# Attention with a memory beside a gated FFN: half blocks of gate and up in row tiles, set-up moved, another order at the end

## The chip, the cores and the metric

The kernel runs on one core of a Trainium2 chip. The metric is device time in microseconds for the whole program, as a median over runs. A profile of one execution is shown beside it.

## The reference, cut to what matters

`x` is 2048 x 448. It is layer-normalised once; both branches read the result.

```python
xn = layernorm(x)
# branch A: 16 heads of 28 features, 4 segments of 512 rows in turn
q, k, v = xn @ wq, xn @ wk, xn @ wv
for s in range(4):
    p = softmax(q_s @ k_s.T * scale + causal_mask)
    a_dot = p @ v_s
    a_mem = (phi(q_s) @ M) / (phi(q_s) @ z + 1e-6)
    o_s = g * a_mem + (1 - g) * a_dot          # g = sigmoid(beta), per head
    M, z = M + phi(k_s).T @ v_s, z + sum(phi(k_s))
s_out = o @ wo
# branch B: w_gate, w_up 448 x 1792, w_down 1792 x 448
ffn = (gelu(xn @ w_gate) * (xn @ w_up)) @ w_down
out = x + s_out * silu(ffn)
```

## The kernel before, in words

All matmuls are bf16 into float32 PSUM. The 448 features stand as `NDC` = 4 chunks of 128 partitions, of which the last holds `DR` = 64 features and 64 rows of zeros. A segment's normalised rows, transposed, are `xnT[s]` (128 x 4 x 512).

The order of all instructions is written out by hand (`manual_schedule`, L79): each engine runs its instructions in the order in which the program issues them. Work goes in stages:

- **Head** (`layer_norm_first`, L265): constants and loads, statistics and transposes of segment 0 by TensorE (`turn`, L253), the four v units between them, then the eight q and k units (`run(units0[:8])`, L623). VectorE writes all set-up zeros first: `fill_constants` (L147) stands ahead of `stats`. 145 matmuls on zeros (L92, L93) keep TensorE at work until then. wq is spread to 32 columns a head by ACT, wk by VectorE (`pad_weight`, L118). `more_loads` (L135) starts the loads of gate, up, down and wo.
- **gate_up(s)** (L477), for s = 0 to 3: 14 blocks `fc` of 128 of the 1792 columns. A block's tile `gu` has two PSUM banks, one for gate and one for up, and there are two such tiles (`ps_s`, shared with the scores). Per block four matmuls for gate and four for up (L484), each 128 rows x 128 weights x 512 columns, then gelu on ACT (L487), the product on VectorE (L488) into `hT[s]`, and then the steps that a table holds for that block: statistics of the next segment (`layer_norm_steps`, L284), the end of the previous attention (`tail`, L632), reads of the memory (`memory`, L637).
- **attention(s, fill, at)** (L556): twelve steps (4 groups of 4 heads x 3 sets of key blocks). Scores are 32-row matmuls, four beside each other in row tiles (L388), exponentials on ACT (L394), the causal mask on GpSimd (L398), PV two steps later in 32-column tiles (L409). A list of other TensorE work (`fill`: q, k, v units, down units, wo units) is dealt out between by estimated costs, and `at` holds steps by half step (24 of them).
- A softmax or memory denominator is gathered by DMA into `dc` (L426), turned into three bf16 terms (`invert`, L435: VectorE, then casts and subtractions on GpSimd or VectorE), sent by DMA into `rows` (L448), and spread over the partitions by a matmul with `spread` (`inverses`, L456). `combine` (L463) and `scale_memory` (L459) multiply by it. This matmul reads all of `rows`, so it waits for every earlier write of it.
- `down_units(s)` (L493): per block of 128 rows 14 matmuls (L499) in five units of 3, 3, 3, 3 and 2, tanh on ACT, a product on VectorE. `finish_units(s)` (L522): four wo matmuls (L528), product and addition, store.
- **End** (L674 to L692): attention 2 carries two of the 20 down units of segment 2, attention 3 the other 18 and two of segment 3. The 18 left over run after it with a table of steps; then the last combine, and the four wo units with their additions on VectorE.

Of the kernel before, what the change touches and what calls it, by code (L numbers as in the profile page):

```python
# [25 lines left out]
def fast_path(tc, A_x, A_wq, A_wk, A_wv, A_wo, A_beta, B_w_gate, B_w_up, B_w_down, out):  # L26
# [16 lines left out]
    with ExitStack() as ctx:  # L43
# [48 lines left out]
        for i in range(145):  # L92
            nc.tensor.matmul(out=idle[:, 0:P], lhsT=wz[:], rhs=wz[:], start=True, stop=True)  # L93
        xns = []
        for i in range(2):
            xns.append(const.tile([P, NDC * P], BF16, name=f"xn{i}"))
            nc.vector.memset(xns[i][:, D:], 0.0)
# [5 lines left out]
        wu_sb = const.tile([P, NDC, F], BF16, name="wu_sb")  # L103
# [14 lines left out]
        def pad_weight(nm):  # L118
            copy = nc.scalar.copy if nm == "wq" else nc.vector.tensor_copy
            copy(out=wpad[nm][:, :, :, 0:Dh], in_=raw[nm][:].rearrange("p c (h d) -> p c h d", d=Dh))  # L120
# [14 lines left out]
        def more_loads():  # L135
            w_dma(nc.sync, wg_sb, B_w_gate)
            w_dma(nc.scalar, wu_sb, B_w_up)
# [4 lines left out]
            nc.sync.dma_start(out=wd_sb[:], in_=B_w_down.rearrange("(c p) n -> p c n", p=P))  # L142
            wo_v = A_wo.rearrange("(g i d) n -> i d g n", i=HG, d=Dh)
            for i in range(HG):
                nc.sync.dma_start(out=wo_sb[i * HP:i * HP + Dh, :, :], in_=wo_v[i])

        def fill_constants():  # L147
            nc.vector.memset(wo_sb[:], 0.0)
            for i in range(2):
                nc.vector.memset(vaug[i][:, :, :, Dh:HP], 0.0)  # L150
                nc.vector.memset(vaug[i][:, :, :, Dh:Dh + 1], 1.0)
            for t in (wg_sb, wu_sb):
                nc.vector.memset(t[DR:P, NDC - 1, :], 0.0)
# [35 lines left out]
        def flush():  # L189

            while waiting:
                tick()
# [37 lines left out]
        def layer_norm(s):  # L230
# [21 lines left out]

            def turn(b):  # L253
# [11 lines left out]
        def layer_norm_first():  # L265
# [3 lines left out]
            fill_constants()  # L269
            pad_weight("wq")  # L270
            for b in range(NB):
                stats(b)
            more_loads()
            units0.extend(project_units(0))
            v = units0[8:]
            for b in range(NB):
                scale_x(b)
                turn(b)
                if b:
                    run(v[b - 1:b])  # L280
            pad_weight("wk")
            run(v[NB - 1:])
# [194 lines left out]
        def gate_up(s, steps):  # L477

            hT[s] = seg2.tile([P, NFC, L], BF16, name="hT")
            for fc in range(NFC):  # L480
                gu = ps_s.tile([P, 2, L], F32, name="s")
                for i, w_sb in enumerate((wg_sb, wu_sb)):
                    for c in range(NDC):
                        nc.tensor.matmul(out=gu[:, i, :], lhsT=w_sb[:, c, fc * P:(fc + 1) * P],  # L484
                                         rhs=xnT[s][:, c, :], start=(c == 0), stop=(c == NDC - 1))
# [137 lines left out]
        run(units0[:8])  # L623
        check = guard()
# [7 lines left out]
        def tail(s, table, ends, n_inv, n_comb, copy=None):  # L632
            in_turn(table, 0, [ends[0], lambda: ends[1](copy)])
            in_turn(table, n_inv, [lambda: invert(s, 0)])
            return in_turn(table, n_comb, [lambda g=g: combine(s, g) for g in range(G)])

        def memory(s, table, n_read, n_inv, n_scale, copy=None):  # L637
            in_turn(table, n_read, [lambda g=g: memory_read(s, g, copy) for g in range(G)])
            in_turn(table, n_inv, [lambda: invert(s, 1)])
# [33 lines left out]
        for s in (2, 3):  # L673
# [3 lines left out]
        ends = attention(2, merge(pu[8:12], pu[:8], finish_units(1)) + d2[:2])  # L677
        at = memory(3, tail(2, {}, ends, 4, 9), 5, 13, 17)
        ends = attention(3, d2[2:] + merge(finish_units(2), d3[:2]), at)
        rest, n = d3[2:], 0  # L680
        fast = dict(eng=nc.vector, queues=[nc.sync, nc.scalar, nc.gpsimd])
        table = {0: [lambda: invert(3, 0, 0, G - 1, nc.vector)], 1: ends[:1], 3: ends[1:],
                 8: [lambda: invert(3, 0, G - 1, G, **fast)]}
        in_turn(table, 6, [lambda g=g: combine(3, g) for g in range(G - 1)])
# [4 lines left out]
        flush()  # L689
        combine(3, G - 1)  # L690
        run(finish_units(3))
        flush()  # L692
# [383 lines left out]
```

## Time and profile before

| | us |
|---|---|
| median of three runs | 295.4 (294.34 to 296.16) |
| the profiled execution | 295.26 |
| its span, from first to last instruction | 293.4 |
| TensorE busy (matmuls) | 261.4 |
| VectorE, ACT, GpSimd busy | 185.5, 157.8, 100.1 |

Engines: PE is TensorE, PEld its weight loads, DVE VectorE, ACT ScalarE, POOL GpSimd, SP SyncE; a name with q is that engine's DMA queue. Lines (L484) are those of the kernel. The profile's slices cut the span into 40 equal parts and give busy tenths; PEclk is TensorE's granted clock in tenths of full speed. The time of a matmul in a row includes its way through the array, so matmuls that follow each other overlap in the records; the distance of their starts is what each costs.

### The profile page before, as it was taken

To read this page: it belongs to the slowest core of one execution; us is meant where nothing else is said; L and a number is where in the kernel's file an instruction comes from. 1 tells how busy PE (TensorE), PEld (TensorE's weight loads), DVE (VectorE), ACT (ScalarE), POOL (GpSimd) and SP (SyncE) were. 2 spreads that over 40 slices of the span, in tenths; PEclk is the share of its full clock that TensorE was granted. 3 is DMA by queue.
4 is the path that set the end of the run, shared out by engine and by line. 5 is a ranking of instruction groups with operands and counts; after the bars stand their busy time and mean duration, and the time that the engine had idled before them with its cause. 6 is when DMAs were issued, how large, how long until landed. Compare 5 with 4: busy or idle time off the path is not lost. (4 is left out here: it accounts for less than half of the span.)

```text
span 293.4 us, 4695 instructions
## 1 busy us (share of the span) xinstructions
PE 261.4 (89%) x1697; PEld 116.9 (40%) x1697; DVE 185.5 (63%) x352; ACT 157.8 (54%) x227; POOL 100.1 (34%) x212
## 2 busy tenths in 40 slices
PE   7789799999999999999999999998999886873770
PEld 7634344433434345444444445443334332231330
DVE  6648666537786787478867654467772585566253
ACT  2338582688985325788853344339896765610000
POOL 4200000145540400976502151304776547550000
PEclk9999999999999999999999999999999998897596
DMA  7997012101010142011110300002000000010002
GB/s 230 349 326 155 19 36 53 49 0 21 19 29 17 29 93 92 12 40 36 35 21 7 72 1 6 7 0 80 17 19 19 4 12 8 32 37 3 2 2 70
DMA packets 26354, 15.11 MB, mean 51 GB/s; under 512 B 17872, under 2 KB 25044, under 8 KB 26324
## 3 DMA queue, kind: packets, MB, share of 16 engines
q1 hardware_dynamic: 23392, 10.20, 14.2%
q10 hardware_dynamic: 2324, 3.16, 3.4%
q0 software_dynamic: 608, 1.38, 1.3%
q8 instruction: 15, 0.25, 0.3%
q14 instruction: 15, 0.12, 0.1%
HBM read 9.18 MB, written 1.84 MB: 38 GB/s over the span
## 5 line engine op out<-in xcount | busy, mean ns | idle before, releaser
L394 ACT ACTIVATE pt<-s 128x1024 bf16<-128x1024 f32 (+1 forms) x96 | 79.3, 886 | 20.1 <-PE s L388 17.9
L398 POOL TENSOR_SCALAR_AFFINE_SELECT pt<-pt 128x256 bf16<-128x256 bf16 x128 | 53.6, 442 | 81.1 <-ACT pt L394 79.6
L487 ACT ACTIVATE gl<-s 128x512 bf16<-128x512 f32 x56 | 33.3, 597 | 58.9 <-PE s L484 41.2
L488 DVE TENSOR_TENSOR hT<-gl,s 128x512 bf16<-128x512 bf16 x56 | 38.5, 687 | 38.1 <-ACT gl L487 37.5
L484 PE MATMUL s<-xnT,wg_sb 128*128 128x512 bf16 x224 | 57.5, 379 | 2.2 <-DVE hT L488 2.2
L484 PE MATMUL s<-xnT,wu_sb 128*128 128x512 bf16 x224 | 57.5, 379 | 0.0
L499 PE MATMUL m<-wd_sb,hT 128*128 128x448 bf16 x224 | 53.9, 375 | 0.0
L484 PEld LDWEIGHTS <-wg_sb 128*128 128x128 bf16 x224 | 21.7, 98 | 28.2 <-issue 3.3
L484 PEld LDWEIGHTS <-wu_sb 128*128 128x128 bf16 x224 | 21.9, 98 | 26.4
L499 PEld LDWEIGHTS <-hT 128*128 128x128 bf16 x224 | 21.4, 102 | 24.4 <-issue 8.5
L388 PE MATMUL s<-qT,kT 32*128 32x512 bf16 (+3 forms) x256 | 22.2, 305 | 3.8 <-ACT pt L394 3.3
L246 POOL TENSOR_TENSOR rstd<-rstd,nhalf 128x2 f32<-128x2 f32 x8 | 5.7, 711 | 50.4 <-DVE rstd L244 50.4
L502 ACT ACTIVATE th<-m 128x448 f32<-128x448 f32 x16 | 8.8, 547 | 25.7 <-PE m L499 25.7
L456 PE MATMUL m<-rows,spread 128*128 128x512 bf16 x28 | 11.5, 417 | 12.2 <-DMA rows<-terms 10.6
L409 PE MATMUL pv<-pt,vaug 128*32 128x512 bf16 (+3 forms) x256 | 17.5, 311 | 0.0
L528 PE MATMUL m<-wo_sb,oT 128*128 128x448 bf16 x64 | 15.0, 355 | 2.3 <-DVE oT L473 1.9
L388 PEld LDWEIGHTS <-kT 32*128 32x128 bf16 x256 | 6.8, 91 | 25.6 <-issue 25.1
L307 PE MATMUL m<-xnT,wq_pad 128*128 128x512 bf16 x64 | 17.0, 380 | 0.0
L307 PE MATMUL m<-xnT,wk_pad 128*128 128x512 bf16 x64 | 16.8, 380 | 0.0
L422 DVE COPY oU<-pv 128x512 f32<-128x512 f32 x14 | 9.6, 684 | 10.4 <-PE pv L409 10.4
L345 PE MATMUL m<-wv_sb,xnT 128*128 128x448 bf16 x64 | 14.7, 353 | 0.6 <-ACT xnT L261 0.5
L311 DVE CAST qT<-m 128x512 bf16<-128x512 f32 x12 | 8.3, 690 | 10.9 <-PE m L307 10.8
(101 smaller groups left out, 291.8 us busy)
## 6 DMA issues: line engine op xcount, KB each, us to landing
x_sb<-in_A_x_dram SPq DMA_DIRECT2D x7, 224.0 KB
wd_sb<-in_B_w_down_dram SPq DMA_DIRECT2D x1, 1568.0 KB
wg_sb<-in_B_w_gate_dram SPq DMA_DIRECT2D x1, 1344.0 KB
wu_sb<-in_B_w_up_dram ACTq DMA_DIRECT2D x1, 1344.0 KB
out_dram<-o_out POOLq DMA_DIRECT2D x12, 112.0 KB, 2.0
xr<-in_A_x_dram ACTq DMA_DIRECT2D x2, 448.0 KB
out_dram<-o_out SPq DMA_DIRECT2D x4, 112.0 KB
wo_sb<-in_A_wo_dram SPq DMA_DIRECT2D x4, 98.0 KB
```

The source lines that it names most:

```text
L307: nc.tensor.matmul(out=pr[:], lhsT=wpad[nm][:, c, g * HG:(g + 1) * HG, :].rearrange("p h d -> p (h d)"), rhs=xnT[s][:, c, :], start=(c == ...
L345: nc.tensor.matmul(out=vp[:, 0:D], lhsT=xnT[s][:, c, b * P:(b + 1) * P], rhs=wv_sb[:, c, :], start=(c == 0), stop=(c == NDC - 1))
L388: nc.tensor.matmul(out=sp[i // 2][:, i % 2, c0:c0 + n], lhsT=kT[s][r, g, kb * P:(kb + 1) * P], rhs=qT[s][r, g, kb * P:L], start=True, stop ...
L394: nc.scalar.activation(out=pt[:, :, 0:w], in_=sp[pr][:, :, 0:w], func=ACT.Exp, scale=scale)
L398: nc.gpsimd.affine_select(out=v, in_=v, pattern=[[0, 2], [1, P]], compare_op=ALU.is_ge, fill=0.0, base=0, channel_multiplier=-1)
L409: nc.tensor.matmul(out=acc[i * HP:(i + 1) * HP, kb * P:L], lhsT=va[:, kb, g * HG + i, :], rhs=pts[i // 2][:, i % 2, c0:c0 + n], start=(kb ...
L456: nc.tensor.matmul(out=r[:], lhsT=spread[:, g, :], rhs=rows[side][:], start=True, stop=True)
L484: nc.tensor.matmul(out=gu[:, i, :], lhsT=w_sb[:, c, fc * P:(fc + 1) * P], rhs=xnT[s][:, c, :], start=(c == 0), stop=(c == NDC - 1))
L487: nc.scalar.activation(out=gl[:], in_=gu[:, 0, :], func=ACT.Gelu_apprx_tanh)
L488: nc.vector.tensor_tensor(out=hT[s][:, fc, :], in0=gl[:], in1=gu[:, 1, :], op=ALU.mult)
L499: nc.tensor.matmul(out=d_ps[:, 0:D], lhsT=hT[s][:, fc, b * P:(b + 1) * P], rhs=wd_sb[:, fc, :], start=(fc == 0), stop=(fc == NFC - 1))
L528: nc.tensor.matmul(out=a_ps[:, 0:D], lhsT=oT[s][:, g, b * P:(b + 1) * P], rhs=wo_sb[:, g, :], start=(g == 0), stop=(g == G - 1))
```

## The change

1. **gate_up:** the last chunk of gate has 64 rows in partitions 0 to 63; the 64 rows of up are put beside them, into partitions 64 to 127 of the same tile (`wu_sb` has three chunks now), and the last 64 features of `xnT` stand in both halves (a further scaling of 64 columns in `scale_x`). Per block three whole matmuls for gate, three for up, and one pair of 64-row matmuls in two row tiles, one for gate and one for up. The pair comes last in even blocks and first in odd ones, so that two pairs meet.
2. **Head:** 78 idle matmuls instead of 145; the memsets of `fill_constants` and the wo load go behind the v units; the zeros of xn, gate and up go away; wq is spread by GpSimd; statistics, scaling and turns in another order, v units after all turns; `flush()` ahead of gate_up.
3. **End:** attention 2 carries eight down units of segment 2, attention 3 the other twelve, six of segment 3 and then the wo units; inversions of that stage on VectorE and in other half steps; 14 units left over, with another table; the last wo by groups into two `ps_s` tiles, three groups ahead of the last combine, and the last additions and stores shared between engines.

```diff
--- before.py
+++ after.py
@@ -89,18 +89,18 @@
         idle = ps_pv.tile([P, L], F32, name="pv")
         wz = const.tile([P, P], BF16, name="wz")
         nc.gpsimd.memset(wz[:], 0.0)
-        for i in range(145):
+        for i in range(78):
             nc.tensor.matmul(out=idle[:, 0:P], lhsT=wz[:], rhs=wz[:], start=True, stop=True)
         xns = []
         for i in range(2):
             xns.append(const.tile([P, NDC * P], BF16, name=f"xn{i}"))
-            nc.vector.memset(xns[i][:, D:], 0.0)
 
         wq_raw = seg2.tile([P, NDC, D], BF16, name="oT")
         wk_raw = seg2.tile([P, NDC, D], BF16, name="oT")
         wv_sb = const.tile([P, NDC, D], BF16, name="wv_sb")
         wg_sb = const.tile([P, NDC, F], BF16, name="wg_sb")
-        wu_sb = const.tile([P, NDC, F], BF16, name="wu_sb")
+
+        wu_sb = const.tile([P, NDC - 1, F], BF16, name="wu_sb")
         wd_sb = const.tile([P, NFC, D], BF16, name="wd_sb")
         wo_sb = const.tile([P, G, D], BF16, name="wo_sb")
         betac = const.tile([P, 1], A_beta.dtype, name="betac")
@@ -116,7 +116,7 @@
             wpad[nm] = const.tile([P, NDC, H, HP], BF16, name=nm + "_pad")
 
         def pad_weight(nm):
-            copy = nc.scalar.copy if nm == "wq" else nc.vector.tensor_copy
+            copy = nc.gpsimd.tensor_copy if nm == "wq" else nc.vector.tensor_copy
             copy(out=wpad[nm][:, :, :, 0:Dh], in_=raw[nm][:].rearrange("p c (h d) -> p c h d", d=Dh))
 
         def pad_columns(nm):
@@ -134,23 +134,20 @@
 
         def more_loads():
             w_dma(nc.sync, wg_sb, B_w_gate)
-            w_dma(nc.scalar, wu_sb, B_w_up)
+            n = (NDC - 1) * P
+            nc.scalar.dma_start(out=wu_sb[:], in_=B_w_up[0:n, :].rearrange("(c p) n -> p c n", p=P))
+            nc.scalar.dma_start(out=wg_sb[DR:P, NDC - 1, :], in_=B_w_up[n:D, :])
             nc.sync.dma_start(
                 out=betac[:],
                 in_=A_beta.rearrange("(h o) -> h o", o=1).unsqueeze(1).to_broadcast([H, RC, 1]))
             load_x(1)
             nc.sync.dma_start(out=wd_sb[:], in_=B_w_down.rearrange("(c p) n -> p c n", p=P))
+
+        def fill_constants():
+            nc.vector.memset(wo_sb[:], 0.0)
             wo_v = A_wo.rearrange("(g i d) n -> i d g n", i=HG, d=Dh)
             for i in range(HG):
                 nc.sync.dma_start(out=wo_sb[i * HP:i * HP + Dh, :, :], in_=wo_v[i])
-
-        def fill_constants():
-            nc.vector.memset(wo_sb[:], 0.0)
-            for i in range(2):
-                nc.vector.memset(vaug[i][:, :, :, Dh:HP], 0.0)
-                nc.vector.memset(vaug[i][:, :, :, Dh:Dh + 1], 1.0)
-            for t in (wg_sb, wu_sb):
-                nc.vector.memset(t[DR:P, NDC - 1, :], 0.0)
             nc.vector.memset(bdmask[:], 0.0)
             for i in range(HG):
                 nc.vector.memset(bdmask[i * HP:i * HP + Dh, i * HP:(i + 1) * HP], 1.0)
@@ -250,6 +247,10 @@
                 nc.vector.tensor_scalar(out=xn[b][:, 0:D], in0=xs[:, b, :], scalar1=mv[:, b, 0:1],
                                         scalar2=rstd[:, b:b + 1], op0=ALU.subtract, op1=ALU.mult)
 
+                nc.vector.tensor_scalar(out=xn[b][:, D:], in0=xs[:, b, D - DR:D],
+                                        scalar1=mv[:, b, 0:1], scalar2=rstd[:, b:b + 1],
+                                        op0=ALU.subtract, op1=ALU.mult)
+
             def turn(b):
                 dst = xnT[s][:, :, b * P:(b + 1) * P]
                 if s > 0:
@@ -266,20 +267,26 @@
             stats, scale_x, turn = layer_norm(0)
             pad_columns("wq")
             pad_columns("wk")
-            fill_constants()
-            pad_weight("wq")
-            for b in range(NB):
+            for b in range(3):
                 stats(b)
             more_loads()
+            pad_weight("wq")
+            scale_x(0)
+            turn(0)
+            scale_x(1)
+            turn(1)
+            stats(3)
+            for i in range(2):
+                nc.vector.memset(vaug[i][:, :, :, Dh:HP], 0.0)
+                nc.vector.memset(vaug[i][:, :, :, Dh:Dh + 1], 1.0)
+            scale_x(2)
+            turn(2)
+            scale_x(3)
+            turn(3)
+            pad_weight("wk")
             units0.extend(project_units(0))
-            v = units0[8:]
-            for b in range(NB):
-                scale_x(b)
-                turn(b)
-                if b:
-                    run(v[b - 1:b])
-            pad_weight("wk")
-            run(v[NB - 1:])
+            run(units0[8:])
+            fill_constants()
 
         def layer_norm_steps(s, table):
 
@@ -479,10 +486,25 @@
             hT[s] = seg2.tile([P, NFC, L], BF16, name="hT")
             for fc in range(NFC):
                 gu = ps_s.tile([P, 2, L], F32, name="s")
-                for i, w_sb in enumerate((wg_sb, wu_sb)):
-                    for c in range(NDC):
-                        nc.tensor.matmul(out=gu[:, i, :], lhsT=w_sb[:, c, fc * P:(fc + 1) * P],
-                                         rhs=xnT[s][:, c, :], start=(c == 0), stop=(c == NDC - 1))
+                cols = slice(fc * P, (fc + 1) * P)
+
+                def whole(start, stop):
+                    for i, w_sb in enumerate((wg_sb, wu_sb)):
+                        for c in range(NDC - 1):
+                            nc.tensor.matmul(out=gu[:, i, :], lhsT=w_sb[:, c, cols],
+                                             rhs=xnT[s][:, c, :], start=start and c == 0,
+                                             stop=stop and c == NDC - 2)
+
+                def halves(start, stop):
+                    for i in range(2):
+                        rs = slice(i * DR, (i + 1) * DR)
+                        nc.tensor.matmul(out=gu[:, i, :], lhsT=wg_sb[rs, NDC - 1, cols],
+                                         rhs=xnT[s][rs, NDC - 1, :], start=start, stop=stop)
+
+                first, second = (whole, halves) if fc % 2 == 0 else (halves, whole)
+                first(True, False)
+                second(False, True)
                 gl = work.tile([P, L], BF16, name="gl")
                 nc.scalar.activation(out=gl[:], in_=gu[:, 0, :], func=ACT.Gelu_apprx_tanh)
                 nc.vector.tensor_tensor(out=hT[s][:, fc, :], in0=gl[:], in1=gu[:, 1, :], op=ALU.mult)
@@ -621,6 +643,7 @@
         units0 = []
         layer_norm_first()
         run(units0[:8])
+        flush()
         check = guard()
 
         def phase(s, table):
@@ -629,14 +652,14 @@
             if s + 2 < NSEG:
                 load_x(s + 2)
 
-        def tail(s, table, ends, n_inv, n_comb, copy=None):
+        def tail(s, table, ends, n_inv, n_comb, copy=None, eng=None):
             in_turn(table, 0, [ends[0], lambda: ends[1](copy)])
-            in_turn(table, n_inv, [lambda: invert(s, 0)])
+            in_turn(table, n_inv, [lambda: invert(s, 0, eng=eng)])
             return in_turn(table, n_comb, [lambda g=g: combine(s, g) for g in range(G)])
 
-        def memory(s, table, n_read, n_inv, n_scale, copy=None):
+        def memory(s, table, n_read, n_inv, n_scale, copy=None, eng=None):
             in_turn(table, n_read, [lambda g=g: memory_read(s, g, copy) for g in range(G)])
-            in_turn(table, n_inv, [lambda: invert(s, 1)])
+            in_turn(table, n_inv, [lambda: invert(s, 1, eng=eng)])
             return in_turn(table, n_scale, [lambda g=g: scale_memory(s, g) for g in range(G)])
 
 
@@ -674,22 +697,38 @@
             xr[s] = x_sb[s]
         ok = nc.values_load(oki[0:1, 0:1], min_val=0, max_val=1)
         pu, d2, d3 = project_units(3), down_units(2), down_units(3)
-        ends = attention(2, merge(pu[8:12], pu[:8], finish_units(1)) + d2[:2])
-        at = memory(3, tail(2, {}, ends, 4, 9), 5, 13, 17)
-        ends = attention(3, d2[2:] + merge(finish_units(2), d3[:2]), at)
-        rest, n = d3[2:], 0
-        fast = dict(eng=nc.vector, queues=[nc.sync, nc.scalar, nc.gpsimd])
-        table = {0: [lambda: invert(3, 0, 0, G - 1, nc.vector)], 1: ends[:1], 3: ends[1:],
-                 8: [lambda: invert(3, 0, G - 1, G, **fast)]}
-        in_turn(table, 6, [lambda g=g: combine(3, g) for g in range(G - 1)])
+        ends = attention(2, merge(pu[8:12], pu[:8], finish_units(1), d2[:8]))
+        at = memory(3, tail(2, {}, ends, 5, 11, eng=nc.vector), 1, 8, 18, eng=nc.vector)
+        ends = attention(3, d2[8:] + d3[:6] + finish_units(2), at)
+
+        v = dict(eng=nc.vector, queues=[nc.sync, nc.scalar, nc.sync])
+        table = {0: [ends[0], lambda: invert(3, 0, 0, G - 1, **v)], 1: ends[1:],
+                 6: [lambda: invert(3, 0, G - 1, G, **v)],
+                 7: [lambda: combine(3, 0)], 8: [lambda: combine(3, 1)], 9: [lambda: combine(3, 2)]}
+        rest = d3[6:]
         for n, u in enumerate(rest):
             run([u])
             for f in table.get(n, ()):
                 f()
         flush()
+        acc = [ps_s.tile([P, 2, L], F32, name="s") for _ in range(2)]
+
+        def wo_part(g):
+            for b in range(NB):
+                nc.tensor.matmul(out=acc[b // 2][:, b % 2, 0:D], lhsT=oT[3][:, g, b * P:(b + 1) * P],
+                                 rhs=wo_sb[:, g, :], start=(g == 0), stop=(g == G - 1))
+
+        for g in range(G - 1):
+            wo_part(g)
         combine(3, G - 1)
-        run(finish_units(3))
-        flush()
+        wo_part(G - 1)
+        for b in range(NB):
+            t = sg.pop((3, b))
+            nc.vector.tensor_tensor(out=t, in0=t, in1=acc[b // 2][:, b % 2, 0:D], op=ALU.mult)
+            o_out = outp.tile([P, D], BF16, name="o_out")
+            add = nc.vector if b % 2 else nc.gpsimd
+            add.tensor_tensor(out=o_out[:], in0=t, in1=xr[3][:, b, :], op=ALU.add)
+            (nc.scalar if b % 2 else nc.sync).dma_start(out=o_v[3][:, b, :], in_=o_out[:])
         return ok
```

## Rows read from the trace of the kernel before

**Rows 1.** The page's busy tenths of TensorE and its granted clock, 40 slices.

```profile
PE   7789799999999999999999999998999886873770
PEclk9999999999999999999999999999999998897596
```

**Rows 2.** Timeline of one gate_up block: start us, us, engine, line, out<-in [idle before].

```profile
37.73 1.03 PE L484 MATMUL s<-xnT,wg_sb 128*128 128x512 bf16 x4
...
38.59 1.03 PE L484 MATMUL s<-xnT,wu_sb 128*128 128x512 bf16 x4
...
39.66 0.60 ACT L487 ACTIVATE gl<-s 128x512 bf16<-128x512 f32 x1 [0.29 <-PE s L484]
...
40.28 0.69 DVE L488 TENSOR_TENSOR hT<-gl,s 128x512 bf16<-128x512 bf16 x1 [0.73 <-ACT gl L487]
```

**Rows 3.** Costliest groups: count | busy us, mean ns | idle us before, releaser.

```profile
L484 PE MATMUL s<-xnT,wg_sb 128*128 128x512 bf16 x224 | 57.5, 379 | 2.2 <-DVE hT L488 2.2
```

**Rows 4.** Windows: stretch; us, busy us by engine (instructions); clock, DMA share, GB/s.

```profile
197.30:225.20 27.90, 25.93 (x196) 9.74 (x193) 17.81 (x28) 23.50 (x30) 18.50 (x40) 1.00 0.11 36
225.20:257.30 32.10, 26.44 (x206) 9.87 (x206) 18.67 (x31) 21.32 (x28) 18.57 (x45) 0.95 0.05 13
257.30:273.10 15.80, 7.51 (x40) 2.79 (x38) 9.99 (x22) 1.09 (x2) 4.15 (x7) 0.84 0.07 19
273.10:289.00 15.90, 11.12 (x43) 4.77 (x43) 8.62 (x14) 1.09 (x2) 0.00 (x0) 0.82 0.07 24
```

**Rows 5.** TensorE's waits in attention 3: us in total, times, longest.

```profile
PE m L456 <- DMA rows<-terms: 2.1, 1, 2.1
```

**Rows 6.** Timeline of the head.

```profile
1.59 10.03 PE L93 MATMUL pv<-wz 128*128 128x128 bf16 x145 [1.59 <-POOL wz L91]
...
4.31 0.38 SPq L68 DMA_DIRECT2D wg_sb<-in_B_w_gate_dram  x1
...
6.94 1.69 ACT L120 COPY wq_pad<-oT 128x1792 bf16<-128x1792 bf16 x1 [4.10 <-DMA oT<-in_A_wq_dram]
...
7.02 0.55 DVE L158 MEMSET rows<- 128x256 uint32 x2
...
7.48 0.57 DVE L240 BATCH_NORM_STATS2 st<-x_sb 128x6 f32<-128x448 bf16 x1
...
11.46 0.61 PE L260 MATMUL m<-ident,xn 128*128 128x128 bf16 x8
...
18.39 0.62 DVE L120 COPY wk_pad<-oT 128x1792 bf16<-128x1792 bf16 x1
...
25.40 1.03 PE L484 MATMUL s<-xnT,wg_sb 128*128 128x512 bf16 x4
```

**Rows 7.** SP's waits in the head.

```profile
SPq L68 <- DMA x_sb<-in_A_x_dram: 0.7, 1, 0.7
```

**Rows 8.** Timeline of TensorE in attention 3: three kinds of matmul in a row.

```profile
253.00 0.54 PE L528 MATMUL m<-wo_sb,oT 128*128 128x448 bf16 x2 [0.40 <-DVE wu_sb L461]
253.47 0.40 PE L388 MATMUL s<-qT,kT 32*128 32x384 bf16 x8
253.80 0.29 PE L409 MATMUL pv<-pt,vaug 128*32 128x256 bf16 x4
```

**Rows 9.** Timeline of the end.

```profile
262.04 0.68 DVE L422 COPY oU<-pv 128x512 f32<-128x512 f32 x1
...
268.49 0.25 DVE L440 TENSOR_SCALAR dc<-dc,igate 32x64 f32<-32x64 f32 x1
...
271.29 0.64 POOL L448 DMA_DIRECT2D rows<-terms  x1 [9.87 <-issue]
...
273.11 0.61 PE L456 MATMUL m<-rows,spread 128*128 128x512 bf16 x1 [5.67 <-DMA rows<-terms]
...
273.50 7.31 PE L499 MATMUL m<-wd_sb,hT 128*128 128x448 bf16 x25
...
288.28 0.63 DVE L536 TENSOR_TENSOR o_out<-wg_sb,x_sb 128x448 bf16<-128x448 f32 x1
```

## The prediction

> **What bounds the kernel now.** I read the slices of the page first: TensorE is at 9 tenths in almost every slice from the sixth to the thirtieth, falls to 7 and 8 at the end, and its granted clock dips only in the last quarter [rows 1]. So up to about 245 us a shorter TensorE stream is a shorter kernel; after that waits matter. The end of the span does not tell where they are, so I read stage by stage.
>
> One block of gate and up: 2 x 4 matmuls of 512 columns, four in 0.862 us (38.59 less 37.73), 0.2155 each, which is 512 columns at 2.4 GHz and 2 ns. The gelu of the block begun at 37.73 starts at 39.66, after the *up* matmuls too; the product ends at 40.97 [rows 2]. TensorE's last column of that block passed at 39.45, so the two-buffer loop is closed 1.52 us later, inside the next block's 1.73: slack 0.2. In all 448 of these matmuls TensorE waited 2.2 us [rows 3]. Gate_up is bound by TensorE, narrowly.
>
> Attention 2 (197.3 to 225.2) has TensorE busy 25.93 of 27.9 us; attention 3 (225.2 to 257.3) 26.44 of 32.1, at a clock of 0.95; the rest is 7.51 of 15.8 and 11.12 of 15.9 [rows 4]. In attention 3 the longest wait is 2.1 us for rows<-terms, the inverses coming back through DMA [rows 5].
>
> **Head.** The last of VectorE's set-up memsets begins at 7.02 and takes 0.55, and the first statistics stand right behind them at 7.48, though SP's wg load, which waits for the same x (0.7 us, [rows 7]), went out at 4.31 [rows 6]. With the vaug, wo, wg, wu, bdmask and rows memsets put off or gone, statistics start at about 4.4. From them to the first transpose took 3.98 us (7.48 to 11.46); now only three blocks' statistics stand ahead instead of four, and GpSimd's power can hide behind one of them only: I estimate 3.2, so 7.6. Of the 145 idle matmuls (1.59 to 11.62) 67 go; at 128 columns and 2.4 GHz, 0.056 each, the rest end at 7.9, so TensorE comes from work at its full level.  But the third and fourth block wait: their power stands on GpSimd behind the moved wq pad, which starts when wq lands (6.94, where ACT's copy starts). Its price on GpSimd is not in the trace. The nearest rows are the same copy on VectorE, 0.62, and on ACT, 1.69; bounds 0.6 and 4 (over twice ACT's). I take 2.2, nearer to ACT's. So 9.2; the power, two scalings with their new 64 columns and two turns, an estimated 2.2 in all from the 3.98 above: v starts at 11.4. Then 16 v matmuls of 448 columns (0.189 each: 3.0 us) and 32 of q and k (6.9) without a break: gate_up at 21.4 instead of 25.4 [rows 6]. Cover at risk: wu's load now goes out some 3 us earlier and shares the DMA engines with wv, and the put-off memsets (2 us of VectorE) delay k's copies. Against that, flush puts all exponentials ahead of the first gelu, and the 2.2 us wait of [rows 3], all in stage 0 by my reading, goes; a wait of about 1.8 for the first gelu takes its place. Head: **-4.4** (-2 to -6).
>
> **Gate and up.** A pair of blocks was 16 matmuls, 3.45 us. Now: 12 whole ones (2.59), two sets of two half-height ones that run beside each other (2 x 0.222), and two changes of the array's tiling. What a change costs is shown where scores and PV meet full matmuls: two of 448 columns begun at 253.00 end at 253.38, the first 32-row matmul starts at 253.47; its 384 and 128 columns (0.21 us at 2.4 GHz) end at 253.68, the next kind starts at 253.80 [rows 8]: 0.1 each. Sum 3.23, gain 0.22 a pair, 28 pairs: 6.2 us. That eight 32-row matmuls, two sets of four on the same rows, need only 0.21 us of stream also says that four run side by side and that the second set's weights load under the first; I take the same for two of 64 rows.
>
> The Trainium skill speaks against this: "TensorE: Matmul & The Clock Gate", Part 3, section "The mechanism", says that a weight load overlaps matmuls in flight only when its row group differs, and the odd block's halves use the row groups of the even block's. By that rule each pair would lose a drain and a load; by the row it does not.
>
> Against the 6.2: memory reads, inverses, PV and the guard are issued after a block; after an even block they fall between the two sets of halves, which makes four changes out of two. By the tables these are block 8 of stage 0, 0, 2, 8, 10, 12 of stage 1, 0, 10, 12 of stage 2, 0, 2, 8, 10 of stage 3: 13 x 0.2 = 2.6. The loop still closes: 1.52 plus a semaphore against 0.2 + 0.44 + 1.3 less the own part, 1.61: slack 0.05, so where VectorE has over 0.9 us of steps a block TensorE waits a little; the work that hid this was the longer block. I add 0.2. Gate_up: **-3.4** (+2 to -6). Dropped memsets are counted above; the extra 64-column scaling hides in VectorE's gaps (0.9 a block).
>
> **Attentions.** Attention 2 takes six more down units, 17 matmuls of 0.189: 3.2 us. TensorE idles 2.0 there [rows 4], in short waits for ACT's exponentials; not all can be filled: **+1.3** (+0.5 to +3.2). Attention 3 has six matmuls fewer (1.1), and the distance from inversion to use grows from 5 to 6 and from 4 to 10 half steps, so the 2.1 us wait [rows 5] goes and with it the clock's dip, 0.05 of 32.1 us at half level for 3.2, some 1.6 us of work. Both inversions' casts go from GpSimd to VectorE, which is busy 18.67 of 32.1 there; I take back an estimated 0.2. **-4.6** (-1 to -7). What is late next: ACT's exponentials.
>
> **Tail.** From the first left-over unit (257.3) to the end of the last add (288.91): 31.6 us. Of this, the last accumulator is copied at 262.04 (+4.7, to +5.4), but its inversion starts only at 268.49, behind two combines; its last DMA is issued on GpSimd at 271.29, and TensorE stands 5.67 us until 273.11 with 25 down matmuls behind it. These take 7.31 us where 25 x 0.189 is 4.7: the 2.6 more is half level (1.2 GHz) for 5.2 us [rows 9]. After: copied by +5.0, 1.8 for the transfer (271.29 to 273.11 is one from issue to use) and 0.1 for the issue: inversion from +6.9; to its last issue 2.2 (2.8 before, the issue on GpSimd an estimated 0.6 late), 1.8 again: inverses at +10.9. All three first combines now read after that write, so TensorE has only units 0 to 7 and the last PVs ahead (5.2 us) and stands 5.7 again, and the clock falls again. Then 3 inverses and 16 down matmuls: 7.25 us at half level, 6.2 if it recovers after 5.2 as before: +17.1. Twelve wo matmuls 2.3, the last inverse and combine 0.4 + 1.4, from the first wo to its product 0.5 (as from a gate block's last matmul, 39.24, to its gelu, 0.42), then 4 products and 2 adds on VectorE (0.62 each; two adds go to GpSimd beside them): +25.4. Four left-over units fewer are in this. **-6.2** (-2 to -9).
>
> **Sum.** -4.4 - 3.4 + 1.3 - 4.6 - 6.2 = -17.3. The profiled execution took 295.26 us (span 293.4, 1.9 around it), 0.05% below the median of 295.4, so no correction: **278.0 us**.
>
> **Rivals.**
> *Halves that do not overlap their loads* (the rule above): per pair a drain and a load, taken as long as two changes, 28 x 0.2 = 5.6: 283.6. Against it the eight matmuls of [rows 8]; for it, that these are 32-row, not 64. Chance 0.12.
> *Waits that stay:* attention 3 finds VectorE or ACT the bound and gains 1 instead of 4.6, or the tail's inverses come 3.5 us later: 281.6. For it: TensorE stands still twice at rows<-terms in the tail, the chain remains, and it now holds back all four combines. Chance 0.22.
> *More than counted:* no half clock after the tail's wait (2.6), the pad on GpSimd at 0.6 (1.6) and attention 3 without further waits (1.4): 272.4. Chance 0.11.
> *Slower than before:* the halves run one after the other, each for its whole modelled 0.38 us: 4 x 0.38 + 0.2 = 1.72 a pair against 0.64 in my sum, 28 x 1.08 = 30: 308. It decides from 0.62 us a pair on (17.3 / 28). Against it [rows 8]. Chance 0.03.
>
> **Numbers.** The forecast has 0.52. 272.4 and 281.6 to 283.6 with their own spread must be reached, 308 not: 271 to 286. A measurement here tells about 1% (3 us) from no change. Faster 0.95, same 0.02, slower 0.03.
>
> **What would show it.** Pairs of blocks 3.23 us apart, halves starting within 10 ns of each other; gate_up's first matmul at 21 to 22; no rows<-terms wait in attention 3, one of 5 to 6 us in the tail with the half level behind it; 25 us from the first left-over unit to the last add. Pairs at 3.45 or more, or a gate_up start after 24, would make it wrong.

## The result, and the profile after

Four runs of the changed kernel took 284.65 us in the median (283.75 to 285.92), four of the kernel before beside them 295.78; the ratio is 0.962 (0.955 to 0.969). The kernel became faster by less than forecast: 6.6 us are missing of 17. The time lies inside the stated range of 271 to 286, near its upper end. The profiled execution took 284.43 us, with a span of 282.6, so the span fell by 10.8.

The page's slices of the changed kernel, to be read against [rows 1]:

```profile
PE   7599999999999899999999989999999989873930
PEclk9989999999999999999999999999999999999795
```

Each slice is 7.07 us now. Attention 3 lost its dip in the clock, the end kept one, and the head got a weak place that it did not have: a 5 in the second slice, an 8 of the clock in the third.

By milestones in the two timelines (first gate_up matmul, first scores of attention 3, last add and so on) the 10.8 us fall to the stages like this. The forecast's -4.4 for the head is split: -4.0 is its earlier start of gate_up (21.4 instead of 25.4), and -0.4 is a wait inside the first gate_up stage (1.8 instead of 2.2), which is counted with gate_up here.

| stage | before | after | change | forecast |
|---|---|---|---|---|
| head, to the first gate_up matmul | 25.40 | 24.64 | -0.8 | -4.0 |
| the four gate_up stages | 108.74 | 105.44 | -3.3 | -3.8 |
| attentions 0 and 1 | 63.2 | 63.2 | 0 | 0 |
| attention 2 | 27.90 | 29.40 | +1.5 | +1.3 |
| attention 3 | 32.04 | 27.68 | -4.4 | -4.6 |
| first left-over unit to the end of the last add | 31.6 | 26.6 | -5.1 | -6.2 |
| last add to the end of the span (the close) | 4.5 | 5.7 | +1.2 | 0 |

The attentions came within 0.2 of the forecast and gate_up within 0.5, the head failed, the end was too hopeful by 1.1, and the last row nobody had priced.

**Gate and up.** The timeline of the first pair of blocks after (the row to compare is [rows 2]):

```profile
24.64 0.81 PE L494 MATMUL s<-xnT,wg_sb 128*128 128x512 bf16 x3
25.29 0.81 PE L494 MATMUL s<-xnT,wu_sb 128*128 128x512 bf16 x3
26.03 0.60 PE L501 MATMUL s<-xnT,wg_sb 64*128 64x512 bf16 x4
26.57 0.82 PE L494 MATMUL s<-xnT,wg_sb 128*128 128x512 bf16 x3
27.23 0.81 PE L494 MATMUL s<-xnT,wu_sb 128*128 128x512 bf16 x3
```

From 25.29, three whole matmuls are 0.65, which ends at 25.94; the halves begin at 26.03: a change of the tiling is 0.1. Four halves last until 26.57 less 0.1, 0.44 for two sets. An undisturbed pair measures 3.235 us, against 3.23 forecast.

**Attention 2, 3 and the end.** Windows (stretch; us, busy us and instructions of PE, PEld, DVE, ACT, POOL; clock, DMA share, GB/s), beside [rows 4]:

```profile
193.30:222.70 29.40, 28.52 (x216) 11.14 (x214) 19.82 (x29) 24.45 (x32) 18.21 (x39) 1.00 0.09 30
222.70:250.40 27.70, 24.13 (x200) 9.12 (x200) 20.93 (x41) 20.62 (x28) 15.47 (x36) 1.00 0.07 19
250.40:262.10 11.70, 5.63 (x37) 2.43 (x36) 7.47 (x17) 1.04 (x3) 4.27 (x8) 1.00 0.09 25
262.10:277.00 14.90, 8.90 (x36) 3.75 (x36) 10.30 (x16) 1.09 (x2) 2.05 (x2) 0.84 0.06 19
```

The six down units moved into attention 2 fill it to 28.5 of 29.4 us. Attention 3 runs at the full clock. In the end the two halves of the problem stand side by side: a stretch in which TensorE waits, and one behind it at a clock of 0.84. The waits of TensorE from attention 3 on (us in total, times, longest) name the reason; the row of [rows 5] is gone from attention 3, and one remains, in the end:

```profile
PE m L463 <- DMA rows<-terms: 5.0, 1, 5.0
```

**The head.** The timeline of the changed kernel, VectorE and GpSimd, to be read against [rows 6]:

```profile
3.89 0.63 DVE L237 BATCH_NORM_STATS2 st<-x_sb 128x6 f32<-128x448 bf16 x1 [1.74 <-DMA x_sb<-in_A_x_dram]
...
6.77 1.68 POOL L120 COPY wq_pad<-oT 128x1792 bf16<-128x1792 bf16 x1 [0.31 <-DMA oT<-in_A_wq_dram]
6.81 1.67 DVE L250 TENSOR_SCALAR xn<-x_sb,mv,rstd 128x64 bf16<-128x64 bf16 x1
...
8.70 0.29 DVE L250 TENSOR_SCALAR xn<-x_sb,mv,rstd 128x64 bf16<-128x64 bf16 x1
8.91 0.62 DVE L237 BATCH_NORM_STATS2 st<-x_sb 128x6 f32<-128x448 bf16 x1
...
10.03 0.69 POOL L243 TENSOR_TENSOR rstd<-rstd,nhalf 128x2 f32<-128x2 f32 x1 [1.58 <-DVE rstd L241]
...
11.24 0.79 DVE L250 TENSOR_SCALAR xn<-x_sb,mv,rstd 128x64 bf16<-128x64 bf16 x1
11.27 2.77 POOL L159 TENSOR_SCALAR_AFFINE_SELECT spread<-spread 128x512 bf16<-128x512 bf16 x3
...
12.24 0.70 DVE L250 TENSOR_SCALAR xn<-x_sb,mv,rstd 128x64 bf16<-128x64 bf16 x1
```

The statistics do start early, at 3.89 instead of 7.48. Then the second of the two scalings of a block, 64 columns that take 0.29 us by themselves (8.70), takes 1.67 while GpSimd spreads wq, and ends with that copy (8.48 and 8.45). Everything behind it on VectorE is late: statistics of the last block at 8.91, so its power on GpSimd (the step that gives rstd) not behind the copy but behind VectorE (the releaser in the 10.03 row), so the third transpose at 11.38. TensorE, whose idle matmuls end at 8.05, shows it:

```profile
8.10 1.18 PE L261 MATMUL m<-ident,xn 128*128 128x128 bf16 x8
11.38 0.34 PE L261 MATMUL m<-ident,xn 128*128 128x128 bf16 x3 [2.10 <-DVE xn L247]
...
13.08 4.82 PE L352 MATMUL m<-wv_sb,xnT 128*128 128x448 bf16 x16
17.74 1.03 PE L314 MATMUL m<-xnT,wq_pad 128*128 128x512 bf16 x4
```

After the wait of 2.1 us the transposes run, then the granted clock is at its half level (1.2 GHz) from 12.96 to 16.38, and the v units take 4.66 us (17.74 less 13.08) instead of 3.0.

### The profile page after: what moved, and what is told of

Same layout as the page of the kernel before. It is cut to its first block, busy times and chain, and to the rows that moved or that the text cites. A ratio compares the mean times of both kernels' runs of the same rounds, so it can differ in the third digit from the quotient of the medians.

```text
span 282.6 us, 4559 instructions
## 1 busy us (share of the span) xinstructions
PE 252.8 (89%) x1630; PEld 105.4 (37%) x1630; DVE 192.2 (68%) x372; ACT 153.9 (54%) x224; POOL 101.2 (36%) x204
## 4 chain that ended last, share of the span: by engine, by line
PE 60%; issue 11%; ACT 11%; POOL 7%; DVE 5%; DMA 5%; ACTq 0%; SPq 0%; POOLq 0%; DVEq 0%
PE s L494 22%; PE m L521 9%; PE m L314 8%; ACT pt L401 7%; PE s L501 5%; PE s L395 4%; PE m L352 4%; PE pv L416 3%; POOL o_out L561 2%; POOL pt L405 2%; DMA oT<-in_A_wq_dram 2%; PE m L463 2%; DMA xnT<-xn 1%; PE m L550 1%; ACT gl L509 1%
## 5 line engine op out<-in xcount | busy, mean ns | idle before, releaser
L401 ACT ACTIVATE pt<-s 128x1024 bf16<-128x1024 f32 (+1 forms) x96 | 79.5, 886 | 17.3 <-PE s L395 15.3
L521 PE MATMUL m<-wd_sb,hT 128*128 128x448 bf16 x224 | 52.0, 360 | 0.2 <-DVE sg L528 0.2
L494 PE MATMUL s<-xnT,wg_sb 128*128 128x512 bf16 x168 | 45.7, 381 | 2.0 <-DVE hT L510 2.0
L494 PE MATMUL s<-xnT,wu_sb 128*128 128x512 bf16 x168 | 45.4, 379 | 0.0
L521 PEld LDWEIGHTS <-hT 128*128 128x128 bf16 x224 | 20.4, 99 | 22.7 <-issue 5.9
L494 PEld LDWEIGHTS <-wu_sb 128*128 128x128 bf16 x168 | 16.4, 98 | 19.9
L395 PE MATMUL s<-qT,kT 32*128 32x512 bf16 (+3 forms) x256 | 21.2, 301 | 2.1 <-ACT pt L401 1.8
L494 PEld LDWEIGHTS <-wg_sb 128*128 128x128 bf16 x168 | 14.1, 97 | 23.0 <-issue 10.8
L501 PE MATMUL s<-xnT,wg_sb 64*128 64x512 bf16 x112 | 19.4, 384 | 0.4 <-DVE hT L510 0.4
L463 PE MATMUL m<-rows,spread 128*128 128x512 bf16 x28 | 10.9, 407 | 5.7 <-DMA rows<-terms 5.3
L352 PE MATMUL m<-wv_sb,xnT 128*128 128x448 bf16 x64 | 15.4, 384 | 0.2 <-DVE vaug L354 0.2
```

Of the source, the lines that this page charges most:

```text
L352: nc.tensor.matmul(out=vp[:, 0:D], lhsT=xnT[s][:, c, b * P:(b + 1) * P], rhs=wv_sb[:, c, :], start=(c == 0), stop=(c == NDC - 1))
L395: nc.tensor.matmul(out=sp[i // 2][:, i % 2, c0:c0 + n], lhsT=kT[s][r, g, kb * P:(kb + 1) * P], rhs=qT[s][r, g, kb * P:L], start=True, stop ...
L401: nc.scalar.activation(out=pt[:, :, 0:w], in_=sp[pr][:, :, 0:w], func=ACT.Exp, scale=scale)
L463: nc.tensor.matmul(out=r[:], lhsT=spread[:, g, :], rhs=rows[side][:], start=True, stop=True)
L494: nc.tensor.matmul(out=gu[:, i, :], lhsT=w_sb[:, c, cols], rhs=xnT[s][:, c, :], start=start and c == 0, stop=stop and c == NDC - 2)
L501: nc.tensor.matmul(out=gu[:, i, :], lhsT=wg_sb[rs, NDC - 1, cols], rhs=xnT[s][rs, NDC - 1, :], start=start, stop=stop)
```

## The experiments

All edits are to the changed kernel; in the tables "g0" is the start of the first gate_up matmul and "last add" the end of the last addition.

### The head: the clock or VectorE beside GpSimd

As many idle matmuls as before:

```diff
-        for i in range(78):
+        for i in range(145):
```

> The changed kernel with 145 idle matmuls again. In the changed kernel's profile TensorE stands still from about 8.3 to 11.4 us, the clock is at half level from 12.96 to 16.38, and the 16 v matmuls take 4.66 us from start to start of q. Theory A (the missing idle matmuls let the clock fall): no half level before 200 us, v in 3.0 us, gate_up's first matmul 1.6 us earlier (24.6 to 23.0), the whole about 283.0. Theory B (the late third and fourth block, that is VectorE beside GpSimd, is all of it): v still at half level or started as much later, gate_up at 24.6, the whole at 284.6.

wq spread by ACT again:

```diff
-            copy = nc.gpsimd.tensor_copy if nm == "wq" else nc.vector.tensor_copy
+            copy = nc.scalar.copy if nm == "wq" else nc.vector.tensor_copy
```

> The changed kernel with wq spread by ACT again, 78 idle matmuls. Theory B (the copy on GpSimd holds up VectorE's 64-column scaling, 1.67 us instead of 0.3, and the power behind it): first scaling 0.3 us, the last transpose at about 12.0 instead of 13.0, gate_up's first matmul 1 us earlier, the whole about 283.6; the half level stays. Theory A alone: the transposes come earlier but TensorE's start is unchanged or the v matmuls fall under the half level for longer: within 0.4 us of 284.6.

| | median us | ratio to before | last transpose | v units | g0 |
|---|---|---|---|---|---|
| changed kernel | 284.65 | 0.962 (0.955 to 0.969) | 13.00 | 4.66 | 24.64 |
| 145 idle matmuls | 283.63 | 0.959 (0.954 to 0.965) | 14.21 | 3.03 | 24.21 |
| wq spread by ACT | 281.51 | 0.955 (0.950 to 0.960) | 11.69 | 3.03 | 21.69 |

More idle matmuls hold the clock and give back the 1.6 us of the v units, but they end at 11.8 and push the transposes behind them: g0 comes only 0.4 earlier. (In the changed kernel TensorE stands for 2.1 us, not from 8.3 on as the expectation has it: until 9.28 it transposes the first two blocks.) With wq on ACT the clock holds too, with 78 idle matmuls, where the expectation had it fall again, and gate_up starts 2.95 us earlier, 0.3 from the forecast's 21.4. VectorE in that run:

```profile
6.58 0.40 DVE L247 TENSOR_SCALAR xn<-x_sb,mv,rstd 128x448 bf16<-128x448 bf16 x1
6.89 0.29 DVE L250 TENSOR_SCALAR xn<-x_sb,mv,rstd 128x64 bf16<-128x64 bf16 x1
7.09 0.39 DVE L247 TENSOR_SCALAR xn<-x_sb,mv,rstd 128x448 bf16<-128x448 bf16 x1
7.40 0.30 DVE L250 TENSOR_SCALAR xn<-x_sb,mv,rstd 128x64 bf16<-128x64 bf16 x1
```

The same instruction, 0.29 instead of 1.67, and all behind it 1.3 us earlier. It need not be the one with 64 columns: in all seven profiles with the copy on GpSimd a scaling takes 1.65 to 1.76 and ends 0.03 to 0.13 behind the copy, a 64-column one in three of them, the 448-column one of the second block (0.39 otherwise) in the other four. So the meeting of the two engines is the cause of the late transposes. Of the 2.95 us, 1.31 are the last transpose (13.00 to 11.69) and 1.64 the v units at the full clock. That the meeting also makes the clock fall is not shown. With 78 idle matmuls and wq on GpSimd it fell in five of the profiles here and stayed in that of the whole blocks below. There the meeting is the same (a scaling takes 1.65, TensorE waits 2.10, the last transpose stands at 12.91). That head differs by two early memsets on GpSimd, and the clock rose to its full level at 7.10 (5.19 to 6.13 in the five), so the idle matmuls ended 0.5 to 0.9 later. The profiled execution of the whole blocks took 285.73 us at a mean granted clock of 0.981, its other three 287.21 to 289.43 at 0.959 to 0.967, so it may change from one execution to the next.

The Trainium skill has the rule that the forecast should have used: "SBUF — State Buffer", section "Who interferes with whom", says that VectorE in certain modes of copies and scalings shares a pair of ports with GpSimd, that the one that comes first holds it for its whole instruction, and that the other stands still meanwhile. The trace agrees: the scaling begins 0.04 behind the copy and ends 0.03 behind its end.

### The half blocks

Whole blocks again, four matmuls of 128 rows for gate and four for up (up in four chunks, the zeros of the last chunks by GpSimd, early):

```diff
-                first(True, False)
-                second(False, True)
+                for i, w_sb in enumerate((wg_sb, wu_sb)):
+                    for c in range(NDC):
...
```

> The changed kernel with gate and up in whole blocks again (eight matmuls of 128 rows; the zeros of the last chunk written by GpSimd ahead of everything). Theory (the half blocks save 0.22 a pair and give back 0.2 wherever a step stands after an even block): blocks 1.728 us apart, the four gate_up stages 3.3 us longer in sum, whole about 288.0. Rival (the loop through gelu and product would have been as fast): whole within 1 us of 284.6.

Half blocks, but the halves last in every block, so that no two sets meet:

```diff
-                first, second = (whole, halves) if fc % 2 == 0 else (halves, whole)
+                first, second = whole, halves
```

> The changed kernel with the two half-height matmuls last in every block, so that no two pairs meet. Theory (each change of tiling costs 0.1 us, nothing else): each block 1.293 + 0.217 + 0.2 = 1.71 instead of 1.62 in blocks without steps; blocks with a step after an even one lose nothing: 15 pairs x 0.2 = 3.0, whole about 287.6. Rival (the loads of the second set are what is hidden by meeting): more than 4 us, since both would be lost.

| | median us | ratio to before | four gate_up stages |
|---|---|---|---|
| changed kernel | 284.65 | 0.962 (0.955 to 0.969) | 105.44 |
| whole blocks | 287.33 | 0.976 (0.972 to 0.980) | 108.56 |
| halves not paired | 286.47 | 0.969 (0.965 to 0.974) | 107.45 |

Whole blocks give back 3.1 of the 3.3 us: the gain of the stage is the half blocks' own. Without the pairing 2.0 are lost, a third less than the 3.0 expected. This is read from one profile of each kernel, since the medians of the two kernels with halves do not lie apart beyond their intervals. The timeline shows the price of a block itself:

```profile
43.77 0.39 PE L501 MATMUL s<-xnT,wg_sb 64*128 64x512 bf16 x2
44.09 0.82 PE L494 MATMUL s<-xnT,wg_sb 128*128 128x512 bf16 x3
44.75 0.81 PE L494 MATMUL s<-xnT,wu_sb 128*128 128x512 bf16 x3
45.49 0.39 PE L501 MATMUL s<-xnT,wg_sb 64*128 64x512 bf16 x2
```

Blocks are 1.72 apart (45.49 less 43.77), hardly less than the whole block's 1.73: two changes of tiling eat what one set of halves saves, and only sets that meet gain. Of the 1.0 by which they lost less than expected, 0.7 is that TensorE waits 1.7 us in all for products of VectorE instead of 2.4; the rest was not followed.

### The end

Everything from attention 2 on as before the change:

```diff
-        ends = attention(2, merge(pu[8:12], pu[:8], finish_units(1), d2[:8]))
+        ends = attention(2, merge(pu[8:12], pu[:8], finish_units(1)) + d2[:2])
...
```

> The changed kernel with everything from attention 2 on as before: down units, half steps, GpSimd's casts, 18 units left over, last wo units. Theory (the stage times of the two profiles: attention 2 +1.5, attention 3 -4.4, left-over units to last addition -5.1, close +1.2 by the change): whole 6.8 us longer, about 291.4. Rival (the earlier start of attention 2 alone removes the waits there): under 3 us.

288.67 us, ratio 0.979 (0.975 to 0.983), against 291.4 expected. From the start of attention 2 to the last add it takes 90.0 us instead of 83.6: these stages lose 6.4, but the span rose by 4.7 and the median by 4.0 only, since the close gives 1.2 back (4.5 instead of 5.7) and the stages ahead were 0.5 shorter in this profile. The change had shortened the three stages by 8.0 in sum; the other 1.6 do not come back with the old end, and why was not followed. TensorE's waits for rows are back in it:

```profile
PE m L463 <- DMA rows<-terms: 11.2, 3, 6.4
```

The close was looked at next: in the changed kernel the last store is issued by ACT at 276.96 and has landed at 279.90, 2.94 us later; before, SP issued the last one at 288.93 and it landed 1.66 later.

```diff
-        outp = pool("outp", 3)
+        outp = pool("outp", 4)
...
-            (nc.scalar if b % 2 else nc.sync).dma_start(out=o_v[3][:, b, :], in_=o_out[:])
+            nc.sync.dma_start(out=o_v[3][:, b, :], in_=o_out[:])
```

> The changed kernel with four buffers for the output instead of three and all four last stores on SP. In the changed profile the last addition waits 0.85 us for the first store, and the last store, issued by ACT at 276.96, lands 2.9 us later, against 1.7 on SP before. Theory (both are real and on the path that ends last): the last instruction before the close comes 2.0 us earlier, whole about 282.6. Rival (the stores share one path and SP's queue takes the time back): 284.0 to 284.6.

283.95 us (0.960; 0.955 to 0.965), no difference that counts. The fourth buffer brings the last add 0.5 us forward, but the store on SP still lands over 3 us after its issue: the queue is not the reason. Among the packets of that stretch are two of 16,384 bytes on a queue that loads instructions. Each holds a DMA engine for 0.9 to 1.7 us, in every profile here. Before the change the first of them (287.21 to 288.42) met the second of the last four stores (3.07 from issue to landing), and the last store, issued at 288.93, landed before the second of them began (290.88). After the change the second one (277.73 to 278.63) meets the last store. That the packets collide is read from their times only; no run took the instruction load away.

Then the wait of 5 us. The left-over units, timeline of the changed kernel:

```profile
253.70 3.39 PE L521 MATMUL m<-wd_sb,hT 128*128 128x448 bf16 x17
262.07 0.55 PE L463 MATMUL m<-rows,spread 128*128 128x512 bf16 x1 [4.98 <-DMA rows<-terms]
262.41 0.95 PE L521 MATMUL m<-wd_sb,hT 128*128 128x448 bf16 x2
```

VectorE had cast the terms of the first three groups at 255.03 already. Their spreading matmuls stood behind the write of the fourth group's rows, whose inversion VectorE ended at 260.05. So the combines were put ahead of that inversion:

```diff
-                 6: [lambda: invert(3, 0, G - 1, G, **v)],
-                 7: [lambda: combine(3, 0)], 8: [lambda: combine(3, 1)], 9: [lambda: combine(3, 2)]}
+                 5: [lambda: combine(3, 0)], 6: [lambda: combine(3, 1)],
+                 7: [lambda: combine(3, 2), lambda: invert(3, 0, G - 1, G, **v)]}
```

> The changed kernel with one table of the end in another order: the three combines stand behind left-over units 5 to 7, and the last group's inversion behind them instead of ahead of them, so that no combine waits for its rows. Theory (the end is held by the second write of rows, since each spreading matmul waits for every earlier write): the rows of the first inversion, cast last at 255.03, are there at about 257.1, when TensorE runs out of units; the three combines take VectorE 257.9 to 262.1, the inversion 262.1 to 264.1, its rows come 1.8 later at 265.9. The 4.98 us wait at 262.07 goes; one of about 1 to 2 us stays ahead of the last spreading matmul, which starts at 266 instead of 269.7, and the last add ends at 273.2 instead of 276.9: 3.7 us less, about 281. If the half level that stands at 262.13 to 265.55 goes too, the matmuls behind it lose no time, but they are not what ends last. Rival: the end is bound by VectorE and the closing stores, and the late store loses what it gains: less than 1.5 us.

280.46 us, ratio 0.948 (0.944 to 0.952), the last add at 272.86: 4.1 less. Timeline of that run:

```profile
257.39 0.38 PE L463 MATMUL m<-rows,spread 128*128 128x512 bf16 x1 [1.42 <-DMA rows<-terms]
...
262.51 2.43 PE L718 MATMUL s<-wo_sb,oT 128*128 128x448 bf16 x12
265.89 0.38 PE L463 MATMUL m<-rows,spread 128*128 128x512 bf16 x1 [0.94 <-DMA rows<-terms]
```

The waits are 1.42 and 0.94, the last spreading matmul starts at 265.89 (266 was expected, 269.69 in the changed kernel), and the clock is at its full level through it all until 268.84. The rival, that the close would eat the gain, falls: it takes 5.7, as in the changed kernel.

### Put together

The wq copy on ACT, `spread` set up early in the head so that GpSimd is idle beside the scalings, four output buffers and stores on SP; first with the old table of the end and 120 idle matmuls, then with the new table and 100:

```diff
             pad_columns("wk")
+            nc.gpsimd.memset(spread[:], 0.0)
...
             for b in range(3):
```

> The changed kernel with 120 idle matmuls, wq spread by ACT, spread's set-up on GpSimd ahead of the statistics, four output buffers and all last stores on SP. If the causes add: head 1.6 + 1.5, end 2.0, so about 279.5. If the clock and the late blocks are one cost seen twice: 281.5.

280.49 us (0.950; 0.947 to 0.954), half way between the two expectations, 279.5 and 281.5, so it decides nothing between them. g0 is at 22.58: 120 idle matmuls end at 10.8 and hold the transposes back.

> The best head of the runs so far (wq spread by ACT, spread set up early by GpSimd, 100 idle matmuls), four output buffers and stores on SP, with the end table in the other order. If the parts add: gate_up starts at about 22.2 (2.4 us before the changed kernel's 24.6), the last add ends 2.4 + 3.7 + 0.5 = 6.6 us before its 276.9, at about 270.3; with the stores' 5.7 the span is 276.0 and the time about 278, against 280.5 of the run with the same head and the old table. Rival (the end gives back): no less than 279.5.

**275.60 us, ratio 0.933 (0.930 to 0.936)**: faster than both kernels. g0 is at 21.33, the last add at 268.96, 1.3 earlier than the sum of the parts, of which 0.9 is the head. VectorE's two last scalings there:

```profile
10.46 0.30 DVE L244 TENSOR_SCALAR xn<-x_sb,mv,rstd 128x64 bf16<-128x64 bf16 x1
...
10.97 0.30 DVE L244 TENSOR_SCALAR xn<-x_sb,mv,rstd 128x64 bf16<-128x64 bf16 x1
```

With `spread` out of their way, they take 0.30 instead of the 0.79 and 0.70 that they take in the changed kernel, and also with wq on ACT, where `spread` is still set up beside them: the sharing shown a second time, with another instruction of GpSimd.

## Why the prediction was right or wrong

**Right: gate and up.** Every term of the pair held: 12 whole matmuls, 0.22 a set, 0.1 a change, halves that start within 10 ns of each other; and in 13 of the 28 pairs the two sets do not meet, as counted. The second set starts 0.23 behind the first on the same row groups, and its weight loads stand at 26.04 and 26.05, 0.01 behind the start of the first set's matmuls: they load under it. The sentence of the Trainium skill that the prediction weighed ("TensorE: Matmul & The Clock Gate", Part 3, "The mechanism": only when the row group differs) does not hold in this trace as it stands; the same section also lets a load into the background weight buffer go ahead, which the prediction left out; with that the trace agrees. Of the 0.5 by which the stages gained less, 0.4 are in the waits for VectorE's products: 2.4 us where the forecast comes to 2.0. It read the 2.2 before the change as all in stage 0, but 1.8 were there, and for after it had 1.8 there and 0.2 elsewhere; measured are 0.8 and about 1.6. The time of 283.6 that the rival of halves that do not overlap gave lies close to what was measured, but not by its mechanism: pairs are at 3.235.

**Right: attention 2 and attention 3**, 0.2 off each; the wait of [rows 5] went, and with it the dip in the clock.

**Wrong: the head**, by 3.2 us, half of what was missing; by the prediction's own sign, a gate_up start after 24, this part is wrong. The step that failed is "the third and fourth block wait: their power stands on GpSimd behind the moved wq pad". The copy took 1.68 on GpSimd, even less than the 2.2 priced, and the power did not wait for it. VectorE did: the forecast put the scalings beside that copy at their own duration. One took 1.67, the statistics of the last block came at 8.91, and TensorE stood for 2.1 us, for which the forecast had no row, since it had the idle matmuls and the transposes follow each other closely. In the sum's terms, the power of the third and fourth block started at 10.03 instead of 9.2 (0.8). From there to the v units it took 3.05 instead of 2.2 (0.85), in part since the two new scalings took 0.79 and 0.70 beside the set-up of `spread`. The v units took 1.6 more at the half clock, for which the forecast had no term; what decides whether the clock falls there stays open. The run with wq on ACT starts gate_up at 21.69, close to the forecast's 21.4 but in part by luck: its power starts at 8.73, 0.5 before the forecast's, and the way from there to the v units takes 3.03, 0.8 more than the forecast's.

**Mis-sized: the end**, by 1.1. The chain of [rows 9] came back as forecast (copy, inversion, rows, one long wait of TensorE, half level behind it), the wait 4.98 for 5.7. The inversion started 7.66 after the first left-over unit instead of 6.9: 0.4 since the copy stands on VectorE behind the first inversion (255.13, where its PV matmuls had ended at 253.77), and 0.3 since SP issued the transfer for it, at 256.22, only behind two for the first inversion; 262.07 is then +11.7 for +10.9. The rest is in the last adds, where VectorE waits 0.85 for an output buffer (0.5 of it came back with four buffers). One subtraction of the first inversion looks like the sharing again:

```profile
252.68 1.83 DVE L454 TENSOR_TENSOR dc<-dc,terms 96x64 f32<-96x64 f32 x1
254.55 0.19 DVE L452 CAST terms<-dc 96x64 bf16<-96x64 f32 x1
254.77 0.22 DVE L454 TENSOR_TENSOR dc<-dc,terms 96x64 f32<-96x64 f32 x1
```

The first of the two equal subtractions runs beside GpSimd's additions and masks and takes 1.83, the second 0.22. No run took that work of GpSimd away. The trace of the kernel before had such a pair already, which the forecast did not use: a cast of 0.19 that takes 1.69 beside GpSimd.

```profile
258.94 1.69 DVE L445 CAST terms<-dc 96x64 bf16<-96x64 f32 x1
259.53 1.03 POOL L539 TENSOR_TENSOR o_out<-sg,x_sb 128x448 bf16<-128x448 f32 x1
260.92 0.19 DVE L445 CAST terms<-dc 96x64 bf16<-96x64 f32 x1
```

**Not priced: the close**, 1.2: the stores were taken to end as late behind the last add as before, and they end later.

Sum of the misses: 3.2 + 0.5 + 0.2 + 0.2 + 1.1 + 1.2 = 6.4 of the 6.5 us by which the span's fall of 10.8 stayed behind the forecast's 17.3 (the rest is rounding). Of the rivals, "waits that stay" (281.6) had the right manner at another place: attention 3 kept no wait, the head got one.

## What to carry to other kernels

An instruction that is moved to an idle engine is not free for the engine beside it: look at what VectorE does while GpSimd works, and take the duration of a VectorE row only from a place where GpSimd is in the same state. Where a matmul reads a whole buffer that is written in parts, issue every use of the first parts ahead of the write of the last one; here that order alone was worth 4.1 us. Halves in row tiles paid here only where two sets meet, since a single set saves 0.21 us and its two changes of the tiling cost 0.2.

## What the runs showed that was not expected

- A VectorE scaling of 128 x 64 took 0.29 us alone and 1.67 beside a copy on GpSimd, a subtraction of 96 x 64 took 0.22 alone and 1.83 beside additions and masks on GpSimd.
- The last store of 112 KB, around which instructions are loaded, lands 2.7 to 3.4 us after its issue in the nine profiles with the new last additions, instead of 1.7, on either queue.
- With 78 idle matmuls and wq on GpSimd, the clock fell to its half level behind a wait of about 2 us in five profiles and not in a sixth, whose head differs by two early memsets; in the run with wq on ACT a wait of 1.26 us left it at the full level.
